# Two of eight pairs of the last batch's first product in seven block products, with changes at the start and the end

## The chip, the core and the metric

The kernel runs on one core of one Trainium2 chip. The core's engines each run their own instructions strictly in order and wait for each other by semaphores: TensorE (PE) multiplies matrices, VectorE (DVE) and ScalarE (ACT) do elementwise work, SyncE (SP) issues most of the transfers, and GpSimd (POOL) does next to nothing here. The metric is the device time of one execution in microseconds (us). The kernel before takes 2216.11 us, the median of three runs (2215.84 to 2216.43).

## The reference

Everything is float32; B is 4, N is 6080, C is 256, F is 2048.

```python
qn = q / (norm(q, axis=1) + 1e-6)          # q, k, v: (4, 6080, 256)
kn = k / (norm(k, axis=1) + 1e-6)
s  = kn.transpose(0, 2, 1) @ qn / tau      # (4, 256, 256): attention over channels
a  = softmax(s)                            # with 1e-9 added to the row sums
x  = (v @ a).reshape(24320, 256)
h  = maximum(x @ w_in, 0)                  # w_in: (256, 2048)
out = (h * h) @ w_out                      # w_out: (2048, 256)
```

## The kernel before

For each batch b the kernel first sums the 256 x 256 products of k and q over all rows (`Gram`), makes the softmax of it, and folds it into the input weights: W = a @ w_in (`softmax_and_W`). Then h = v @ W replaces two products. The weights of a batch are in four groups g of 512 columns; v comes in twelve blocks n of rows (ten of 512, two of 480).

Float32 operands are split into a high part that TensorE takes in one go and a low remainder (`_hi`, `_lo`), and each product is made of three: hi·hi, hi·lo, lo·hi. ACT makes the high part (a cast), DVE the low part (a subtraction).

The main loop (lines 798 to 849) runs over `steps` (b, n, f), with f one of 16 slices of 128 columns of h; two slices are a pair r (0 to 7). A step has `first_product` (lines 579 to 594): six matmuls of 512 columns into one of the three PSUM tiles of the pool `ps_h` (`bufs=3`, line 98), which ACT then empties by a relu into half of the tile `x` of the pair. Tiles of `x`, `g_hi` and `g_lo` have two buffers each. After the second step of a pair `squares_and_sums` (603) squares `x` on ACT, has DVE make four differences and sums of its quarters (slots 4 to 7), and splits slots 1 to 3 into `g_hi` and `g_lo`; one step later `parts_of_sums` (616) splits slots 4 to 7, ACT by a cast of 1024 columns and DVE by a subtraction of 1024.

The second product (h² @ w_out) is made two pairs later (`LAG = 2`): for blocks between the first two and the last (`by_seven`, 572) by seven products of 128 x 128 blocks instead of eight (`seven_products`, 651; sums of w_out are made once, in `sums_of_w_out`), nine matmuls of 256 columns in the pair's first step and twelve in its second. For the others it is `eight_products` (707). After a block's last pair ACT copies the two PSUM tiles `ps_o` (768 and 1024 columns) to SBUF, which frees them for the next block, DVE combines them over three later steps (`combine`), and SP stores them. Beside this, in each block, v of the next block is split (ACT at f = 6, DVE at f = 8) and v of the one after is loaded.

For the batches 1 to 3 the generator `attention_of_others` does the Gram products, softmax and W of the next batch piece by piece in between; during batch 3 nothing is left of that but the end of W. At the start `start_first` (310) loads nine chunks of q and k of batch 0 ahead on SP, TensorE sums their products, ACT squares them and DVE adds the squares up for the norms. The order that follows until the first W is written out by hand in `beside_first`, and `stages` times the decoding of the weights (they come as float64 and are decoded on ACT and DVE).

The lines on which the working turns are those that order a pair's work:

```python
if part == 0 and 0 <= i // 2 - 1 < len(pairs):
    parts_of_sums(*pairs[i // 2 - 1])
...
if part == 1 and i // 2 < len(pairs):
    squares_and_sums(*pairs[i // 2])
...
if i >= 2 * LAG:
    second_product(*pairs[i // 2 - LAG], part)
```

## Time and profile before

| | |
|---|---|
| median of three runs | 2216.11 us |
| the profiled execution | 2216.45 us |
| its span, first to last instruction | 2214.6 us |
| granted TensorE clock | 1.000 |
| ACT busy, share of the span | 83% |
| DVE busy, share of the span | 79% |
| transfers | 127 MB, 57 GB/s on average |

In the rows of the profile an engine's instructions are named by the tile written and the tiles read, with the shape as partitions x elements. All compute instructions carry line 27, that of a helper, so they are told apart by tile names. A timeline row begins with the start and the duration in us; in brackets stands the idle time ahead of it and what ended that. On ACT and DVE the recorded durations of independent neighbours overlap by some 0.1 us, so what an instruction takes of its engine is read from the distance of two starts.

### The profile page before, as it was taken

The numbers are of one execution on the slowest core, as the hardware profiler recorded it, in microseconds if no ns is written. First come the engines' busy times: TensorE is split into PE (matmuls) and PEld (weight loads), VectorE is DVE, ScalarE is ACT, GpSimd is POOL, SyncE is SP. The second block draws the span as 40 slices with busy tenths as digits, with TensorE's granted clock in tenths as the row PEclk, the third lists the DMA queues.
The fourth block names the chain that finished last, engine by engine and source line by source line (L and its number), as shares of the span: only waits on it lengthen the run. The fifth ranks groups of instructions, "written<-read, shape, count | busy, mean of one in ns | idle before, by whom it ended". The sixth has DMA issues, their size and how long they took to land.

```text
span 2214.6 us, 34388 instructions
## 1 busy us (share of the span) xinstructions
PE 2206.4 (100%) x13750; PEld 1982.2 (90%) x13750; DVE 1759.8 (79%) x2469; ACT 1842.3 (83%) x2294; POOL 0.7 (0%) x6
## 2 busy tenths in 40 slices
PE   9999999999999999999999999999999999999999
PEld 8788999989989999998998999998899888888898
DVE  6878888888778888878767888888877777777773
ACT  5788888888788888888878888888887888888885
POOL 0000000000000000000000000000000000000000
PEclk9999999999999999999999999999999999999999
DMA  9521122101111122110121222110102010010000
GB/s 342 179 77 38 60 75 67 46 19 38 57 67 58 61 70 70 55 41 22 36 76 48 69 64 69 58 53 23 37 20 76 21 37 20 22 36 20 22 26 18
DMA packets 76496, 127.01 MB, mean 57 GB/s; under 512 B 7728, under 2 KB 35120, under 8 KB 76336
## 3 DMA queue, kind: packets, MB, share of 16 engines
q1 hardware_dynamic: 76336, 124.81, 17.3%
q8 instruction: 108, 1.77, 0.3%
q14 instruction: 52, 0.43, 0.1%
HBM read 95.68 MB, written 29.10 MB: 56 GB/s over the span
## 4 chain that ended last, share of the span: by engine, by line
PE 98%; DVE 1%; DMA 0%; ACT 0%; issue 0%; SPq 0%; DVEq 0%
PE ps_h L27 47%; PE ps_o L27 43%; PE gram L27 6%; PE ps_w L27 2%; DVE dec_m L27 0%; DMA qk<-in_q 0%; DMA w_raw<-in_w_in 0%; PE ps_n L27 0%; DVE wi_lo L27 0%; ACT x L27 0%; ACT g_hi L27 0%; DVE w_lo L27 0%; PE ps_t L27 0%; PE ps_b L27 0%; DVE g_lo L27 0%
## 5 line engine op out<-in xcount | busy, mean ns | idle before, releaser
L27 DVE TENSOR_TENSOR g_lo<-x,g_hi 128x768 fp32r<-128x768 f32 (+2 forms) x744 | 804.2, 1081 | 97.2 <-ACT g_hi L27 96.5
L27 DVE TENSOR_TENSOR x<-x 128x256 f32<-128x256 f32 (+3 forms) x1080 | 550.8, 510 | 274.5 <-ACT x L27 249.1
L27 ACT CAST g_hi<-x 128x768 fp32r<-128x768 f32 (+2 forms) x744 | 697.8, 938 | 25.0 <-DVE x L27 12.2
L27 ACT ACTIVATE x<-ps_h 128x512 f32<-128x512 f32 (+1 forms) x768 | 455.7, 593 | 289.7 <-PE ps_h L27 266.0
L27 PE MATMUL ps_h<-v_hi,w_hi 128*128 128x512 f32 (+1 forms) x1536 | 478.5, 393 | 0.0
L27 PE MATMUL ps_h<-v_hi,w_lo 128*128 128x512 f32 (+1 forms) x1536 | 477.8, 392 | 0.0
L27 PE MATMUL ps_h<-v_lo,w_hi 128*128 128x512 f32 (+1 forms) x1536 | 475.0, 390 | 0.8 <-DVE v_lo L27 0.8
L27 ACT ACTIVATE x<-x 128x1024 f32<-128x1024 f32 (+1 forms) x384 | 404.4, 1053 | 11.9
L27 PE MATMUL ps_o<-g_lo,wS_hi 128*128 128x256 f32 (+1 forms) x1440 | 401.9, 279 | 0.0
L27 PE MATMUL ps_o<-g_hi,wS_lo 128*128 128x256 f32 (+1 forms) x1440 | 401.2, 279 | 0.0
L27 PE MATMUL ps_o<-g_hi,wS_hi 128*128 128x256 f32 (+1 forms) x1440 | 400.4, 278 | 0.0
L27 PEld LDWEIGHTS ps_h<-v_lo,w_hi 128*128 128x128 f32 x1536 | 287.8, 187 | 65.9 <-DVE v_lo L27 1.2
L27 PEld LDWEIGHTS ps_h<-v_hi,w_lo 128*128 128x128 f32 x1536 | 288.5, 188 | 62.4 <-DVE w_lo L27 0.3
L27 PE MATMUL ps_o<-g_hi,wo_hi 128*128 128x256 f32 (+3 forms) x1176 | 330.9, 288 | 0.0
L27 PE MATMUL ps_o<-g_hi,wo_lo 128*128 128x256 f32 (+3 forms) x1176 | 330.7, 288 | 0.0
L27 PE MATMUL ps_o<-g_lo,wo_hi 128*128 128x256 f32 (+3 forms) x1176 | 330.5, 288 | 0.0
L27 PEld LDWEIGHTS ps_o<-g_lo,wS_hi 128*128 128x128 f32 x1440 | 271.0, 188 | 15.9 <-DVE g_lo L27 0.2
L27 PEld LDWEIGHTS ps_o<-g_hi,wS_hi 128*128 128x128 f32 x1440 | 270.3, 188 | 15.5
L27 PEld LDWEIGHTS ps_o<-g_hi,wS_lo 128*128 128x128 f32 x1440 | 270.6, 188 | 0.0
L27 PEld LDWEIGHTS ps_h<-v_hi,w_hi 128*128 128x128 f32 x1536 | 238.9, 188 | 5.3
L27 PEld LDWEIGHTS ps_o<-g_hi,wo_hi 128*128 128x128 f32 x1176 | 221.5, 188 | 16.4
L27 PEld LDWEIGHTS ps_o<-g_lo,wo_hi 128*128 128x128 f32 x1176 | 220.8, 188 | 16.6 <-DVE g_lo L27 0.3
(90 smaller groups left out, 1668.1 us busy)
## 6 DMA issues: line engine op xcount, KB each, us to landing
qk<-in_k SPq DMA_DIRECT2D x87, 256.0 KB, 2.7
qk<-in_q SPq DMA_DIRECT2D x87, 256.0 KB, 3.0
v<-in_vT SPq DMA_DIRECT2D x40, 512.0 KB, 3.7
out_T<-o SPq DMA_DIRECT2D x152, 128.0 KB, 1.7
wi_hi<-wi_kept SPq DMA_DIRECT2D x12, 512.0 KB, 3.3
...
```

The lines of the kernel that those rows point to most:

```text
L27: return lambda *args, **kwargs: self.tc.keep_in_program_order(issue(*args, **kwargs))
```

## The change

In batch 3, for the blocks 2 to 10, the pairs r = 1 and r = 5 make their h by seven block products too. With v's block in quarters B and W's slice in quarters A, four sums S of the A and four sums T of the B are made, and the pair's two steps take 12 and 9 matmuls of 256 columns instead of 6 and 6 of 512. `sums_of_W` makes S once per pair (after W of batch 3 is done), `sums_of_v` and `parts_of_v_sums` make T for each block, a block ahead (at f = 8, 12, 14 and 15). The sums that such a product needs behind it are made in PSUM: ACT copies the first product out, and four DVE instructions add it and its followers up, before the second step's nine matmuls accumulate on top. For such a pair the order of the step changes: the pair before it has its differences made after this, and in the pair's second step the second product of an earlier pair comes first.

At the start, q's chunks 0 to 3 are issued by ACT instead of SP, tau is loaded after the chunks, and ACT's first activation (which loads its function table) comes behind its five transfers. In the first W the low part's products of both halves come last, with two pieces of the next batch's Gram ahead of them; in the later three W of batch 0 that second part comes behind the second product. v_lo of block 1 is made ahead of the weights' decoding. In the blocks 1 to 9 of batch 3, v_lo of the next block and the load behind it move from f = 8 to f = 13. At the end, the last block's sums lie in two PSUM tiles instead of one, the two copies go to separate SBUF tiles, and the second half is stored by ACT's queue.

```diff
@@ start @@
-    nc.sync.dma_start(tau_sb, tau.to_broadcast([P, 1]))
...
-    scalar.activation(const.tile([P, 1], F32, name="first"), exp_bias, AF.Square)
...
+            other = scalar if self.b == 0 and c < 4 else nc.sync
             for j0, j1 in pieces:
                 nc.sync.dma_start(raw[:p, 1, j0:j1, :], self.k[c][2][:, j0:j1, :])
-                nc.sync.dma_start(raw[:p, 0, j0:j1, :], self.q[c][2][:, j0:j1, :])
+                other.dma_start(raw[:p, 0, j0:j1, :], self.q[c][2][:, j0:j1, :])
...
         for c in range(AHEAD):
             load(c)
+        nc.sync.dma_start(tau_sb, tau.to_broadcast([P, 1]))
+        scalar.activation(const.tile([P, 1], F32, name="first"), exp_bias, AF.Square)
@@ softmax_and_W @@
-                for h, terms in ((0, (0, 1)), (1, (0,)), (0, (2,)), (1, (1, 2))):
+                for h, terms in ((0, (0, 1)), (1, (0, 1))):
                     products(h, terms)
                 yield
+                for h in range(NC):
+                    products(h, (2,))
                 for h in range(NC):
                     evict(h)
...
+        if b == B - 1:
+            for r in SEVEN_FIRST:
+                yield from sums_of_W(b, r)
+    SEVEN_FIRST, FIRST = (1, 5), 2
@@ the sums of v @@
+        if piece == 0:
+            vector.tensor_sub(S[:, 0:3:2, :], raw[:, :, half:tn], raw[:, 0, :tn].rearrange("p (k t) -> p k t", k=2))
+        else:
+            vector.tensor_sub(S[:, 1, :], raw[:, 1, half:tn], S[:, 0, :])
+            vector.tensor_sub(S[:, 3, :], raw[:, 1, 0:half], S[:, 1, :])
...
+        if part:
+            vector.tensor_sub(to, S, VS[b, n][1].bitcast(F32))
+        else:
+            scalar.copy(to, S)
@@ seven_first_products @@
+            for i, (wt, vt) in enumerate(((A[0], B_[0]), (A[0], B_[1]), (A[1], B_[0]))):
+                tensor.matmul(ps, wt, vt, start=start and i == 0, stop=stop and i == 2, skip_group_check=True)
...
+        if part == 0:
+            x = X[b, n, r] = pool.tile([P, 8, half], F32, tag="x", name=f"x{b}_{n}_{r}")
+            one, two = H[b, n, r] = [
+                ps_h.tile([P, 2, T // 2], F32, tag="h", name=f"ps_h{b}_{n}_{r}_{i}")[:, :, :half] for i in range(2)
+            ]
+            product(one[:, 0], "A11", "B11", start=True)
+            product(one[:, 1], "S2", "T2", stop=True)
+            product(two[:, 0], "S1", "T1", start=True)
+            product(two[:, 1], "S3", "T3")
+            P1, U4, U2 = (x[:, i, :] for i in (4, 5, 6))
+            scalar.copy(P1, one[:, 0])
+            vector.tensor_add(U2, one[:, 1], P1)
+            vector.tensor_add(U4, two[:, 0], U2)
+            vector.tensor_add(x[:, 3, :], two[:, 1], U4)
+            vector.tensor_add(two, two, x[:, 6:7, :].broadcast_to([P, 2, half]))
+        else:
+            product(one[:, 0], "A12", "B21", stop=True)
+            product(two[:, 0], "S4", "B22")
+            product(two[:, 1], "A22", "T4", stop=True)
+            scalar.activation(x[:, 3, :], x[:, 3, :], AF.Relu)
+            scalar.activation(x[:, 0, :], one[:, 0], AF.Relu)
+            scalar.activation(x[:, 1:3, :], two, AF.Relu)
@@ the end @@
+            tiles = [
+                ps_acc.tile([P, NC, T], F32, tag="o", name=f"ps_o{b}_{n}_{i}") for i in range(NC if final else 1)
+            ]
...
+            if last:
+                for tag, m, copy, queue in (("acc", 0, scalar.copy, nc.sync), ("dec", 1, vector.tensor_copy, scalar)):
+                    o = pool.tile([P, tn], F32, tag=tag, name=f"o{b}_{n}_{tag}", bufs=1)
+                    copy(o, psum[m])
+                    queue.dma_start(out[:, m, :], o)
+                return
@@ the main loop @@
+        chained, chain_next = (j < len(steps) and first_by_seven(*steps[j]) for j in (i, i + 1))
+        chain_next = chain_next and part == 1
+        if chained and part:
+            second_product(*pairs[i // 2 - LAG], part)
...
+            if i == 1:
+                split_v_lo(*order[1])
             for item in stages.get(i, ()):
                 weights.stage(item)
-            if i == 1:
-                split_v_lo(*order[1])
...
+        if chained and part == 0:
+            sums_and_parts(*pairs[i // 2 - 1])
         if part == 0 and 0 <= i // 2 - 1 < len(pairs):
             parts_of_sums(*pairs[i // 2 - 1])
-        if i in steps_of_W:
-            next(first)
         if part == 1 and i // 2 < len(pairs):
-            squares_and_sums(*pairs[i // 2])
+            squares(*pairs[i // 2])
+            if not chain_next:
+                sums_and_parts(*pairs[i // 2])
...
-        if i >= 2 * LAG:
+        if i >= 2 * LAG and not (chained and part):
             second_product(*pairs[i // 2 - LAG], part)
+        if i in steps_of_W:
+            next(first)
...
-            at_hi, at_lo = (None, None) if at == 0 else (12, 13) if at == 1 else (6, 8)
+            then = at + 1 < len(order) and has_sums(*order[at + 1])
+            at_hi, at_lo = (None, None) if at == 0 else (12, 13) if at == 1 else (6, 13) if then else (6, 8)
```

ACT's instructions of batch 3, block 5, from pair 0's second relu to pair 2's first, before. In the names 3_5_1 is batch 3, block 5, pair 1 (for `ps_h` the last number is the slice f, for `ps_o` and `o` there is only the block, and part 0 or 1); the number behind is that of the tile.

```order
L27 ACTIVATE x3_5_0_18843<-ps_h3_5_1_18856 128x512
L27 ACTIVATE x3_5_0_18843<-x3_5_0_18843 128x1024
L27 CAST g_hi3_5_0_18864<-x3_5_0_18843 128x768
L27 ACTIVATE x3_5_1_18891<-ps_h3_5_2_18884 128x512
L27 CAST g_hi3_5_0_18864<-x3_5_0_18843 128x1024
L27 COPY o3_4_18904<-ps_o3_4_0_18542 128x768
L27 ACTIVATE x3_5_1_18891<-ps_h3_5_3_18906 128x512
L27 ACTIVATE x3_5_1_18891<-x3_5_1_18891 128x1024
L27 CAST g_hi3_5_1_18914<-x3_5_1_18891 128x768
L27 COPY o3_4_18904<-ps_o3_4_1_18569 128x1024
L27 ACTIVATE x3_5_2_18942<-ps_h3_5_4_18935 128x512
```

The same stretch of ACT in the changed kernel; `ps_h3_5_1_0` and `ps_h3_5_1_1` are the two PSUM tiles of pair 1.

```order
L27 ACTIVATE x3_5_0_18983<-x3_5_0_18983 128x1024
L27 COPY x3_5_1_19017<-ps_h3_5_1_0_19018 128x256
L27 CAST g_hi3_5_0_19037<-x3_5_0_18983 128x768
L27 CAST g_hi3_5_0_19037<-x3_5_0_18983 128x1024
L27 COPY o3_4_19055<-ps_o3_4_0_18660 128x768
L27 COPY o3_4_19055<-ps_o3_4_1_18688 128x1024
L27 ACTIVATE x3_5_1_19017<-x3_5_1_19017 128x256
L27 ACTIVATE x3_5_1_19017<-ps_h3_5_1_0_19018 128x256
L27 ACTIVATE x3_5_1_19017<-ps_h3_5_1_1_19019 128x512
L27 ACTIVATE x3_5_1_19017<-x3_5_1_19017 128x1024
L27 CAST g_hi3_5_1_19083<-x3_5_1_19017 128x768
L27 ACTIVATE x3_5_2_19098<-ps_h3_5_4_19091 128x512
```

The two relus of 512 columns have become a copy ahead of pair 0's casts and three relus behind both copies of `ps_o`; between pair 0's two casts nothing else is left.

DVE at the same place, before: the last subtraction of block 4, then the sums and low parts of pair 0 and the sums of pair 1.

```order
L27 TENSOR_TENSOR g_lo3_4_7_18817<-x3_4_7_18795,g_hi3_4_7_18816 128x768
L27 TENSOR_TENSOR g_lo3_4_7_18817<-x3_4_7_18795,g_hi3_4_7_18816 128x1024
L27 TENSOR_TENSOR x3_5_0_18843<-x3_5_0_18843 128x512
L27 TENSOR_TENSOR x3_5_0_18843<-x3_5_0_18843 128x256 x2
L27 TENSOR_TENSOR g_lo3_5_0_18865<-x3_5_0_18843,g_hi3_5_0_18864 128x768
L27 TENSOR_TENSOR g_lo3_5_0_18865<-x3_5_0_18843,g_hi3_5_0_18864 128x1024
```

DVE there in the changed kernel; `vS1` is the low part of T, `vS0` its high part.

```order
L27 TENSOR_TENSOR g_lo3_4_7_18956<-x3_4_7_18931,g_hi3_4_7_18955 128x768
L27 TENSOR_TENSOR vS13_5_18974<-v_sums3_5_18777,vS03_5_18944 128x1024
L27 TENSOR_TENSOR g_lo3_4_7_18956<-x3_4_7_18931,g_hi3_4_7_18955 128x1024
L27 TENSOR_TENSOR x3_5_1_19017<-ps_h3_5_1_0_19018,x3_5_1_19017 128x256
L27 TENSOR_TENSOR x3_5_1_19017<-ps_h3_5_1_1_19019,x3_5_1_19017 128x256 x2
L27 TENSOR_TENSOR ps_h3_5_1_1_19019<-ps_h3_5_1_1_19019,x3_5_1_19017 128x512
L27 TENSOR_TENSOR x3_5_0_18983<-x3_5_0_18983 128x512
L27 TENSOR_TENSOR x3_5_0_18983<-x3_5_0_18983 128x256 x2
L27 TENSOR_TENSOR g_lo3_5_0_19038<-x3_5_0_18983,g_hi3_5_0_19037 128x768
L27 TENSOR_TENSOR g_lo3_5_0_19038<-x3_5_0_18983,g_hi3_5_0_19037 128x1024
```

Four instructions of pair 1 now stand ahead of the three sums of pair 0, on whose result ACT's cast of 1024 columns waits.

More of the change, by code (lines that the diff above doesn't have):

```diff
@@ L347, in rest @@
         def rest():
-            for c in range(g.n - LAST, g.n):
-                for _ in g.products(c, [(g.raws[c], g.raws[c])]):
-                    pass
+            for _ in first_products:
+                pass
             yield
@@ L544, in softmax_and_W, with blocks_of_W, sums_of_W @@
             yield
+        if b == B - 1:
+            for r in SEVEN_FIRST:
+                yield from sums_of_W(b, r)
+    SEVEN_FIRST, FIRST = (1, 5), 2
+    WS = {}
+    def blocks_of_W(b, r):
+        f0 = 2 * (r % PPG) * P
+        return [[[w[:, j, f0 + i * P : f0 + (i + 1) * P] for j in range(2)] for i in range(2)] for w in W[b, r // PPG]]
+    def sums_of_W(b, r):
+        f0 = 2 * (r % PPG) * P
+        hi, lo = (w[:, :, f0 : f0 + 2 * P].bitcast(F32) for w in W[b, r // PPG])
+        room = pool.tile([P, 2, NC, 2 * P], F32, tag="acc", name=f"w{b}_{r}", bufs=1)
+        w = room[:, 0]
+        S = room[:, 1].rearrange("p j (i m) -> p (j i) m", i=2)
+        vector.tensor_add(w, hi, lo)
+        yield
+        A11, A12, A21, A22 = (w[:, j, i * P : (i + 1) * P] for i in range(2) for j in range(2))
+        S1, S2, S3, S4 = (S[:, i] for i in range(4))
+        vector.tensor_add(S1, A21, A22)
+        vector.tensor_sub(S3, A11, A21)
+        yield
+        vector.tensor_sub(S2, S1, A11)
+        vector.tensor_sub(S4, A12, S2)
+        yield
+        both = pool.tile([P, 2, 4, P], F32R, tag="qk", name=f"WS{b}_{r}", bufs=QK_BUFS)
+        WS[b, r] = both[:, 0], both[:, 1]
+        scalar.copy(both[:, 0], S)
+        yield
+        vector.tensor_sub(both[:, 1], S, both[:, 0].bitcast(F32))
+        yield
     may_write_W = {(0, g) for g in range(NG)}
@@ L577, with has_sums, first_by_seven, seven_first_products @@
     G = {}
+    H = {}
+    def has_sums(b, n):
+        return b == B - 1 and FIRST <= n < NB - 1
+    def first_by_seven(b, n, f):
+        return has_sums(b, n) and f // 2 in SEVEN_FIRST
+    def seven_first_products(b, n, r, part):
+        half = blocks[n][1] // 2
+        _, v_hi, v_lo = V[b, n]
+        def product(ps, a, b_, start=False, stop=False):
+            A, B_ = W_of[a], v_of[b_]
+            for i, (wt, vt) in enumerate(((A[0], B_[0]), (A[0], B_[1]), (A[1], B_[0]))):
+                tensor.matmul(ps, wt, vt, start=start and i == 0, stop=stop and i == 2, skip_group_check=True)
+        A = blocks_of_W(b, r)
+        W_of = {f"A{i + 1}{j + 1}": [a[i][j] for a in A] for i in range(2) for j in range(2)}
+        W_of.update({f"S{i + 1}": [p[:, i, :] for p in WS[b, r]] for i in range(4)})
+        v_of = {
+            f"B{j + 1}{k + 1}": [v[:, j, k * half : (k + 1) * half] for v in (v_hi, v_lo)] for j in range(2) for k in range(2)
+        }
+        v_of.update({f"T{i + 1}": [p[:, i, :] for p in VS[b, n][1:3]] for i in range(4)})
+        if part == 0:
[14 more added lines that the diff above has]
+        else:
+            one, two = H.pop((b, n, r))
+            x = X[b, n, r]
+            product(one[:, 0], "A12", "B21", stop=True)
[4 more added lines that the diff above has]
+            scalar.activation(x[:, 1:3, :], two, AF.Relu)
@@ L709, in eight_products @@
         f = 2 * r + part
+        final = (b, n) == order[-1]
         if f == 0:
-            O[b, n] = ps_acc.tile([P, NC, T], F32, tag="o", name=f"ps_o{b}_{n}")
+            tiles = [
+                ps_acc.tile([P, NC, T], F32, tag="o", name=f"ps_o{b}_{n}_{i}") for i in range(NC if final else 1)
+            ]
+            O[b, n] = [tiles[m % len(tiles)][:, m, :tn] for m in range(NC)]
         hi, lo = (x.rearrange("p s t -> p (s t)")[:, part * tn : (part + 1) * tn] for x in G[b, n, r])
@@ L714, in eight_products @@
         order_of = [(i, m) for i in range(3) for m in range(NC)]
-        last = (b, n, f) == steps[-1]
+        last = final and f == NF - 1
         if last:
@@ L729, in eight_products @@
         if f == NF - 1:
-            o = pool.tile([P, NC, tn], F32, tag="o_sb", name=f"o{b}_{n}", bufs=1)
             at = b * N + t0
@@ L846 @@
                     load_v(*order[at + 2])
+            if then and f in (14, 15):
+                parts_of_v_sums(*order[at + 1], f - 14)
         if i >= PAIR and part:
```

50 lines of the change are left out of this document (34 added, 16 removed).

## The prediction

> **What bounds the kernel now.** I read the page first: its span, its busy times and its chain of waits.
>
> ```profile
> span 2214.6 us, 34388 instructions
> PE 2206.4 (100%) x13750; PEld 1982.2 (90%) x13750; DVE 1759.8 (79%) x2469; ACT 1842.3 (83%) x2294; POOL 0.7 (0%) x6
> PE 98%; DVE 1%; DMA 0%; ACT 0%; issue 0%; SPq 0%; DVEq 0%
> ```
>
> TensorE is busy all the time and is 98% of the chain: each matmul less is a gain, so long as the others keep up. They have to be asked in the stage that is changed, batch 3 from about 1750 us on. TensorE's timeline there gives the pace; below are the first rows of four stretches that follow each other.
>
> ```profile
> 1800.71 0.28 PE L27 MATMUL ps_o<-g_hi,wo_hi 128*128 128x256 f32 x1
> ...
> 1801.77 0.62 PE L27 MATMUL ps_h<-v_hi,w_hi 128*128 128x512 f32 x2
> ...
> 1803.15 0.28 PE L27 MATMUL ps_o<-g_hi,wS_hi 128*128 128x256 f32 x1
> ...
> 1804.55 0.40 PE L27 MATMUL ps_h<-v_hi,w_hi 128*128 128x512 f32 x1
> ```
>
> The distance of starts tells the cost, as durations overlap: nine matmuls of 256 columns take 1.06 us, six of 512 take 1.38, twelve of 256 take 1.40, so 0.117 for 256 columns and 0.231 for 512. A pair is 2 x 1.38 + 1.06 + 1.40, about 5.24 us with rounding, a block of eight 41.9.
>
> Then ACT's and DVE's timelines over some pairs of the same stage.
>
> ```profile
> 1787.65 0.60 ACT L27 ACTIVATE x<-ps_h 128x512 f32<-128x512 f32 x1 [0.81 <-PE ps_h L27]
> 1788.29 1.06 ACT L27 ACTIVATE x<-x 128x1024 f32<-128x1024 f32 x1
> 1789.38 0.83 ACT L27 CAST g_hi<-x 128x768 fp32r<-128x768 f32 x1
> 1790.45 0.60 ACT L27 ACTIVATE x<-ps_h 128x512 f32<-128x512 f32 x1 [0.23 <-PE ps_h L27]
> 1791.03 1.05 ACT L27 CAST g_hi<-x 128x1024 fp32r<-128x1024 f32 x1
> 1792.89 0.60 ACT L27 ACTIVATE x<-ps_h 128x512 f32<-128x512 f32 x1 [0.81 <-PE ps_h L27]
> ...
> 1797.21 0.79 ACT L27 COPY o<-ps_o 128x768 f32<-128x768 f32 x1
> ...
> 1800.58 1.01 ACT L27 COPY o<-ps_o 128x1024 f32<-128x1024 f32 x1
> 1801.49 0.60 ACT L27 ACTIVATE x<-ps_h 128x512 f32<-128x512 f32 x1
> ...
> 1807.68 1.04 ACT L27 CAST v_hi<-v 128x1024 fp32r<-128x1024 f32 x1
> 1808.63 0.59 ACT L27 ACTIVATE x<-ps_h 128x512 f32<-128x512 f32 x1
> ```
>
> ```profile
> 1789.38 1.61 DVE L27 TENSOR_TENSOR x<-x 128x512 f32<-128x512 f32 x3 [1.28 <-ACT x L27]
> 1790.91 0.95 DVE L27 TENSOR_TENSOR g_lo<-x,g_hi 128x768 fp32r<-128x768 f32 x1
> 1792.11 1.23 DVE L27 TENSOR_TENSOR g_lo<-x,g_hi 128x1024 fp32r<-128x1024 f32 x1 [0.25 <-ACT g_hi L27]
> ...
> 1813.53 1.22 DVE L27 TENSOR_TENSOR g_lo<-x,g_hi 128x1024 fp32r<-128x1024 f32 x1
> 1814.66 1.22 DVE L27 TENSOR_TENSOR v_lo<-v,v_hi 128x1024 fp32r<-128x1024 f32 x1
> ```
>
> ACT waits for TensorE twice in a pair, 0.81 and 0.23. Without these waits a pair has a shortest round, which hangs on both engines: relu to square 0.64, square to DVE's three sums 1.09, sums 1.61, and only then ACT's cast of 1024, which holds ACT 0.95 (from the v_hi row to the next). That is **4.3 us against TensorE's 5.24**: behind by some delay, ACT makes up 0.9 in each pair. The block's extras are two copies of ps_o (0.7 and 0.91) and v_hi (0.95). So before, ACT's round of a block is 8 x 4.3 + 2.6 = 37.0 of 41.9: room of 4.9 us.
>
> **The seven products, on TensorE.** For a pair r = 1 or 5, twelve matmuls of 512 columns (2.77 us) give way to 21 of 256 (2.45): 0.32 us. Nine blocks with two pairs each: 18 x 0.32 = **-5.8 us**. A block is then 41.3.
>
> **The seven products, on ACT and DVE.** Not in the trace are ACT's copies and relus of 256 columns out of PSUM and DVE's adds that read and write PSUM. The nearest rows are these.
>
> ```profile
> L27 ACT COPY o<-ps_o 128x512 f32<-128x512 f32 x4 | 2.1, 586 | 0.0
> L27 ACT ACTIVATE s<-s,negmax 128x256 f32<-128x256 f32 x8 | 4.0, 500 | 0.9 <-DVE negmax L27 0.9
> L27 DVE TENSOR_TENSOR eT_lo<-ps_t,eT_hi 128x512 fp32r<-128x512 f32 x4 | 2.8, 691 | 0.1
> L27 DVE TENSOR_TENSOR x<-x 128x256 f32<-128x256 f32 x608 | 258.4, 425 | 20.8
> ```
>
> From 512 to 1024 columns ACT's copy grows by 0.42, so 256 take about 0.37 (at most the 0.50 of the second row). A DVE subtraction from PSUM takes 0.69, which is also what the first of the three sums leaves of 1.61 after two of 0.425, so I take 0.42 for 256 columns and 0.69 for the 512 written back to PSUM.
>
> What counts is not these durations but where they stand. In ACT's new order the copy of 256 follows pair 0's square, and pair 0's cast of 1024 waits for three sums that DVE now makes behind four instructions of pair 1. These four depend on each other and on the copy: 3 x 0.42 + 0.69 + 3 x 0.04 = 2.1 us. I count from pair 0's second relu (0): square 0.64 to 1.7, copy to 2.0, the four to 4.1, the three sums to 5.6, the cast to 6.65. From the cast of 768 (done by 2.7) to 5.6 ACT has nothing it may do: behind the waiting cast stand both copies of ps_o and pair 1's relus, and TensorE waits for the PSUM tiles that these set free. Then three relus (0.27 + 0.27 + 0.64), square at 7.7, sums to 10.4, cast, and the next relu at 11.4. **Two pairs take 11.4 instead of 8.6.**
>
> A block of ACT is then 4 ordinary pairs (17.2), 2 x 11.4 = 22.8, the old extras 2.6 and the high part of v's sums 0.95: 43.5 us. DVE's additions come in its way at three places: the low part of v's sums (1.13) delays the subtraction that frees pair 1's tile x (0.55), v's first sum of the next block and the combining stand ahead of the four in pair 5 (0.6), and v's later sums ahead of pair 6's (0.4). That makes **45.1 us against TensorE's 41.3**, so ACT and DVE bound these blocks, and the saving on TensorE is lost.
>
> How it reaches TensorE: in block 2 ACT is still on time. In pair 1 TensorE, counted from its first product, needs the emptied ps_o at 6.3 and the emptied first tile at 7.4, and ACT gives them at 6.35 and 7.8: 0.5 us. ACT is then 2.6 us late, makes up 3 x 0.9 less v_hi's 0.95 until pair 5, where the four adds end about 1.1 us after TensorE wants to add to their tile, and 0.1 us more is lost at a low part: 1.2. So block 2 costs 1.7 - 0.64 = +1.1. From block 3 on ACT never catches up: 45.1 - 41.9 = +3.2 each for seven blocks, 22.4, and about +2.8 for block 10 with 480 columns. **Sum: +26.** Without the three collisions (1.55 a block) it would be 14, with 0.3 more for each pair's new instructions 31.
>
> Making S once per pair of weights (two adds, a copy and a subtraction of 512 columns, four adds of 256) costs DVE some 3 us each, spread over steps ahead of block 2. The later row is from there:
>
> ```profile
> 1800.00:1840.00 40.00, 40.00 (x252) 35.85 (x251) 31.66 (x46) 33.48 (x42) 0.00 (x0) 1.00 0.09 27
> ...
> 1740.00:1760.00 20.00, 20.00 (x130) 18.04 (x129) 13.86 (x20) 16.75 (x21) 0.00 (x0) 1.00 0.00 1
> ```
>
> (columns: stretch, length, busy PE, its weight loads, DVE, ACT, POOL, then clock, DMA share, GB/s). DVE has 6 of 20 us free there, so I take nothing; at worst a late tile costs 1 us once. The later load of v lands within a few us and has nine steps of 2.6 before it is read: nothing.
>
> **The start.** The issues on SP and TensorE's Gram in the timeline, then two stretches of 1 us with what the transfers moved:
>
> ```profile
> 0.74 0.38 SPq L106 DMA_DIRECT2D tau_sb<-in_tau  x1
> 1.18 0.42 SPq L267 DMA_DIRECT2D qk<-in_k  x1
> ...
> 3.54 0.44 SPq L268 DMA_DIRECT2D qk<-in_q  x1
> ...
> 8.73 39.09 PE L27 MATMUL gram<-qk 128*128 128x256 f32 x180 [1.48 <-DMA qk<-in_q]
> ```
>
> ```profile
> 4.00:5.00 1.00, 1.00 (x4) 0.69 (x4) 0.00 (x0) 0.00 (x0) 0.00 (x0) 1.00 0.67 150
> ...
> 9.00:10.00 1.00, 1.00 (x6) 0.88 (x5) 0.24 (x1) 0.76 (x2) 0.00 (x0) 1.00 1.03 391
> ```
>
> From 8.73 TensorE runs 39 us without a stop, and what it waits for is q's chunk 1, the sixth of SP's issues (3.54). The issues are 0.47 apart; with tau behind and q's on ACT, chunk 1's q is the third of ACT's queue, issued some 1.8 us earlier. But between 4 and 9 us the engines move less than the 391 GB/s later, and not each dip need be want of issues. Tau's place alone (0.44) is the least, the full 1.8 of earlier issue the most; I take **-1.3**, in the upper half because two thirds of that bandwidth lie idle in the worst dip. The earlier Gram also needs the squares' additions to come earlier, which follow the same transfers. ACT's table load moves behind five issues; its first square waits for chunk 0 anyhow.
>
> The Trainium skill's page "DMA: Bandwidth & Descriptors", section "Issuing engines are not separate DMA queues", says that a second issuing engine saves only the time of issuing, since all transfers share the same 16 engines. By that, up to 1.8 us of issue are to be had and none of the bandwidth; the trace agrees in so far as the engines are not full until 9 us, and a term of -1.8 would move the sum by half a us.
>
> **The first W and the end.** TensorE's waits, and ACT's and DVE's last copies:
>
> ```profile
> PE ps_h L27 <- DVE v_lo L27: 0.8, 1, 0.8
> PE ps_w L27 <- DVE wi_lo L27: 0.5, 1, 0.5
> ```
>
> ```profile
> 2210.33 0.56 ACT L27 COPY o<-ps_o 128x480 f32<-128x480 f32 x1 [3.94 <-PE ps_o L27]
> ...
> 2210.93 0.66 DVE L27 COPY o<-ps_o 128x480 f32<-128x480 f32 x1 [3.34 <-ACT o L27]
> ```
>
> v_lo ahead of the decoding and W's last part behind the second product take away 1.3 at best. Against it, a piece of Gram that stood between the first W and h stands ahead now, so TensorE waits there for ACT's w_hi, up to 1 us. I take **-0.5**, between -1.3 and +1. At the end DVE need not wait for ACT's copy: **-0.6**, the transfer behind it unchanged. In return block 11 needs both tiles of ps_o at once instead of one: 0 to 1 us, **+0.2**, as ACT has the sums of only one kind of pair less there and catches up.
>
> **The sum**, from the profiled execution's own 2216.45 us (0.3 over the median shown): 2216.45 + 26 - 1.3 - 0.5 - 0.6 + 0.2 = about **2240 us**.
>
> **Rivals.** *The waits stay hidden* (faster): ACT's added work is 0.6 us a seven pair and 0.95 a block, so its busy time rises from 35.1 a block (33.48 of 40) to some 37 of 41.3, DVE's from 33.2 to about 39.8. If three PSUM tiles and two of each SBUF tile carry ACT over its empty 2.9 us, only the saving is left: 2216.45 - 5.8 - 1.3 - 0.5 - 0.6 + 0.1 = 2208.4. It decides where ACT's round falls below 41.3, that is with 1.9 us less per seven pair. For it speaks that neither engine is full; against it that each row of the walk is a wait in program order, which a spare buffer doesn't shorten.
>
> The Trainium skill's page "Perfetto Trace Analysis", section "Identifying the Most-Contended Engine", calls occupancy a fair measure for ACT and DVE of how near they are to their limit. By that rule this rival holds, since both stay under 97%; but in this case's rows DVE stands idle 1.28 and 0.25 in each pair, both times for ACT, and such waits in a round of two engines are in no occupancy.
>
> *ACT catches up in each block* (same): the stall is that of pair 1 alone, 9 x 0.5 = 4.5: 2208.4 + 4.5 = 2212.9. It needs the adds in PSUM to be done 1 us sooner than I count. *The 21 matmuls are no faster*, if 256 columns took 0.132 there: 5.8 more on TensorE, but then ACT's bound hides it; no time of its own.
>
> **How the numbers follow.** My forecast has 0.66, with a range of its own from 2227 (no collisions) to 2247 (dearer new instructions). The hidden waits have 0.22, ACT catching up 0.12. A measurement of this kernel can tell about 0.2% (4.4 us) from no change: faster below 2211.7, slower over 2220.5. So faster 0.22, same 0.12, slower 0.66. To leave out no more than 2 in 10 the range must reach into the faster case: 2208 to 2247.
>
> **What would show it.** In the blocks 3 to 9 the distance of equal rows of TensorE should be about 45 us; in pair 0 of each, ACT should sit idle some 2.9 us ahead of its cast of 1024 for DVE, and TensorE's waits name ACT's x and DVE's ps_h. If TensorE has no waits after 1800 us and the blocks are 41.3 apart, the walk is wrong. Chunk 1's Gram should start near 7.4 and not 8.73, DVE's last copy near the last matmul.

## The result, and the profile after

| | before | after |
|---|---|---|
| median of the runs | 2215.98 us (2215.45 to 2216.43, 4 runs) | 2249.23 us (2248.14 to 2249.49, 4 runs) |
| profiled run, its span | 2216.45, 2214.6 us | 2249.34, 2247.5 us |
| ratio after to before | | 1.0148, 95% interval 1.0136 to 1.0160 |

The change makes the kernel 1.5% slower, 33 us; the forecast was 24 (2240 us, range 2208 to 2247). The direction and the mechanism were right; the size lies outside the range, because block 2, the round of a block and the changes ahead of the blocks were each priced too low.

The page of the kernel after: span, busy times and the shares of the chain of waits.

```profile
span 2247.5 us, 34867 instructions
PE 2214.8 (99%) x13912; PEld 1987.1 (88%) x13912; DVE 1818.0 (81%) x2589; ACT 1846.4 (82%) x2341; POOL 0.7 (0%) x6
PE 85%; DVE 8%; ACT 6%; DMA 1%; issue 0%; ACTq 0%; DVEq 0%; SPq 0%
```

TensorE's share of the chain falls from 98% to 85%, though "busy" still says 99%: its busy time is 8.4 us longer than before, with less to multiply, so the profile records part of its waiting as busy. What it waits for is in the list of TensorE's waits of the kernel after (total us, times, longest):

```profile
PE ps_h L27 <- DVE v_lo L27: 7.8, 8, 1.0
PE ps_o L27 <- ACT o L27: 7.6, 9, 0.9
PE ps_h L27 <- DVE ps_h L27: 6.8, 9, 1.1
...
PE ps_h L27 <- ACT x L27: 1.8, 9, 0.2
PE ps_o L27 <- ACT g_hi L27: 1.4, 1, 1.4
```

The four that come 8 or 9 times stand once in each block with seven products (a "seven block" from here on); before, these blocks had none of them. Together they are 24.0 us, less than is lost: at the pace read below, eight blocks lose 4 us each against TensorE's own 41.3. Where they come from is seen in ACT's timeline around pairs 0 and 1 of block 4:

```profile
1888.44 0.37 ACT L27 COPY x<-ps_h 128x256 f32<-128x256 f32 x1 [0.56 <-DVE g_lo L27]
1888.71 0.84 ACT L27 CAST g_hi<-x 128x768 fp32r<-128x768 f32 x1
1892.53 1.05 ACT L27 CAST g_hi<-x 128x1024 fp32r<-128x1024 f32 x1 [2.99 <-DVE x L27]
1893.49 1.70 ACT L27 COPY o<-ps_o 128x768 f32<-128x768 f32 x2
1895.09 0.42 ACT L27 ACTIVATE x<-x 128x256 f32<-128x256 f32 x1
1895.40 0.87 ACT L27 ACTIVATE x<-ps_h 128x256 f32<-128x256 f32 x2
```

and in DVE's for the same time:

```profile
1888.84 1.41 DVE L27 TENSOR_TENSOR x<-ps_h,x 128x256 f32<-128x256 f32 x3 [0.49 <-ACT x L27]
1890.29 0.70 DVE L27 TENSOR_TENSOR ps_h<-ps_h,x 128x512 f32<-128x512 f32 x1
1890.90 1.60 DVE L27 TENSOR_TENSOR x<-x 128x512 f32<-128x512 f32 x3
```

ACT stands still for 2.99 us ahead of pair 0's cast of 1024; meanwhile DVE does pair 1's four adds (2.06 from 1888.84) and only then pair 0's three sums. The copies of ps_o and pair 1's relus stand behind the waiting cast, and TensorE needs the tiles that they empty. ACT's pace is read from ACT's copies of 256 columns, of pair 1 in blocks 2, 3 and 10:

```profile
1797.57 0.37 ACT L27 COPY x<-ps_h 128x256 f32<-128x256 f32 x1 [0.42 <-PE ps_h L27]
...
1843.00 0.37 ACT L27 COPY x<-ps_h 128x256 f32<-128x256 f32 x1 [0.56 <-DVE g_lo L27]
...
2160.80 0.36 ACT L27 COPY x<-ps_h 128x240 f32<-128x240 f32 x1 [0.57 <-PE ps_h L27]
```

Eight blocks in 363.2 us are 45.40 us each, and the very first takes 45.43.

In the lead-in, TensorE's timeline of the kernel after shows the first W and the first product with w_out, which waits for ACT where before it did not:

```profile
62.56 1.27 PE L27 MATMUL ps_w<-wi_lo,eT_hi 128*128 128x512 f32 x4
64.14 1.08 PE L27 MATMUL ps_h<-v_hi,w_hi 128*128 128x512 f32 x2 [0.32 <-ACT w_hi L27]
...
73.91 0.73 PE L27 MATMUL ps_o<-g_hi,wo_hi 128*128 128x512 f32 x2 [1.38 <-ACT g_hi L27]
```

### The profile page after: what moved, and what is told of

The parts are those of the page before. It is cut to its first block, busy times and chain, and to the rows that moved or that the text cites. A ratio compares the mean times of both kernels' runs of the same rounds, so it can differ in the third digit from the quotient of the medians.

```text
span 2247.5 us, 34867 instructions
## 1 busy us (share of the span) xinstructions
PE 2214.8 (99%) x13912; PEld 1987.1 (88%) x13912; DVE 1818.0 (81%) x2589; ACT 1846.4 (82%) x2341; POOL 0.7 (0%) x6
## 4 chain that ended last, share of the span: by engine, by line
PE 85%; DVE 8%; ACT 6%; DMA 1%; issue 0%; ACTq 0%; DVEq 0%; SPq 0%
PE ps_h L27 41%; PE ps_o L27 37%; PE gram L27 5%; DVE x L27 4%; ACT x L27 3%; PE ps_w L27 2%; ACT g_hi L27 2%; DVE g_lo L27 2%; DMA qk<-in_q 1%; ACT o L27 1%; DVE acc L27 1%; DVE v_sums L27 0%; DVE v_lo L27 0%; DVE o L27 0%; ACT v_hi L27 0%
## 5 line engine op out<-in xcount | busy, mean ns | idle before, releaser
L27 ACT ACTIVATE x<-ps_h 128x512 f32<-128x512 f32 (+2 forms) x768 | 449.1, 587 | 234.1 <-PE ps_h L27 212.4
L27 PE MATMUL ps_h<-v_lo,w_hi 128*128 128x512 f32 (+2 forms) x1500 | 463.5, 388 | 7.8 <-DVE v_lo L27 7.8
L27 PE MATMUL ps_h<-v_hi,w_hi 128*128 128x512 f32 (+2 forms) x1500 | 468.8, 391 | 2.2 <-ACT x L27 1.8
L27 PE MATMUL ps_h<-v_hi,w_lo 128*128 128x512 f32 (+2 forms) x1500 | 466.1, 389 | 0.0
L27 ACT ACTIVATE x<-x 128x1024 f32<-128x1024 f32 (+3 forms) x402 | 411.6, 1024 | 11.9
L27 PEld LDWEIGHTS ps_h<-v_lo,w_hi 128*128 128x128 f32 x1500 | 280.3, 187 | 73.5 <-DVE v_lo L27 11.2
L27 PEld LDWEIGHTS ps_h<-v_hi,w_lo 128*128 128x128 f32 x1500 | 281.8, 188 | 59.2
L27 PEld LDWEIGHTS ps_h<-v_hi,w_hi 128*128 128x128 f32 x1500 | 233.9, 188 | 9.8 <-ACT x L27 3.6
```

Source lines behind the costliest of these rows:

```text
L27: return lambda *args, **kwargs: self.tc.keep_in_program_order(issue(*args, **kwargs))
```

## The experiments

Theory A: the order on ACT and DVE in pairs 0/1 and 4/5 makes their round of a block longer than TensorE's, and the loss is there. Rivals: the amount of work, the matmuls of 256 columns, v_lo's move, or the start. Behind each run's edit stands what was expected of it; the cuts of code show the lines that matter.

### The two halves apart: no_seven and only_seven

no_seven takes the pairs out of the changed kernel:

```
-    SEVEN_FIRST, FIRST = (1, 5), 2
+    SEVEN_FIRST, FIRST = (), 2
     def has_sums(b, n):
-        return b == B - 1 and FIRST <= n < NB - 1
+        return False
```

only_seven puts the changed start, W order and end back to those of before and keeps the pairs.

> The changed kernel with no pair of seven products and none of the sums made for them; its start, its first W and its end stay as changed. Theory A (the round of ACT and DVE in the seven pairs, 45.4 us a block against the 41.9 before, costs some 31 us): what is left is the lead-in, 2.9 us later in the trace of the changed kernel, less 0.5 at the end, so about 2218.4 us. Rival (the loss comes from the start or is a general slowing): well over 2225 us.

> The kernel before with the two pairs of seven products alone; start, first W and end as before. Theory A: the two parts of the change add up, so 2216.0 + 31 = about 2247 us, blocks 3 to 9 at 45.4 us each. Rival (the seven pairs suffer from what the start or the W order does to them): clearly under 2245 us.

no_seven: 2218.83 us (10 runs, 1.0013 of before, 1.0004 to 1.0022). only_seven: 2247.12 us (1.0141, 1.0124 to 1.0158). The seven products cost 31.2 us (2247.12 - 2215.88, the median of before beside it); the rest of the change costs 3.0.

### Order or work: no_adds and sums_first

no_adds leaves out ACT's copy of the first product and the four adds; one DVE copy of 256 columns stands in their place:

```
-            scalar.copy(P1, one[:, 0])
-            vector.tensor_add(U2, one[:, 1], P1)
-            vector.tensor_add(U4, two[:, 0], U2)
-            vector.tensor_add(x[:, 3, :], two[:, 1], U4)
-            vector.tensor_add(two, two, x[:, 6:7, :].broadcast_to([P, 2, half]))
+            vector.tensor_copy(x[:, 3, :], two[:, 1])
```

sums_first issues the three sums of the pair ahead at another place and nothing else:

```
             scalar.copy(P1, one[:, 0])
+            sums_of_h(*pairs[pairs.index((b, n, r)) - 1])
             vector.tensor_add(U2, one[:, 1], P1)
...
-            sums_and_parts(*pairs[i // 2 - 1])
+            sums_and_parts(*pairs[i // 2 - 1], summed=True)
```

> The changed kernel without ACT's copy of the first product and with one DVE copy of 256 columns (some 0.42 us) in the place of the four adds that follow each other (2.1 us): the sums of the products of h are left out, everything else is issued as before. Theory A (DVE's chain stands ahead of pair 0's sums): two pairs of a block fall by 2 x 1.7 us at least, the block from 45.4 to 42.1 or to TensorE's own 41.3, so 2212 to 2220 us. Rival (the 21 products of 256 columns or v_lo's later place cost the time): 2245 us or more, the block still over 45 us.

> The changed kernel with the same instructions in another order: DVE makes pair 0's three sums ahead of the four adds of the seven pair, and ACT's copy of the first product stays ahead of the cast of 768. Theory A (order, not work): the adds end 1.3 us later but the cast of 1024 no longer waits for them; two pairs take some 10.6 us rather than 11.4, a block 1.6 less than 45.4, so about 2235 us (2230 to 2241). Rival (the sum of the work on ACT and DVE sets the pace): no change, 2249 us.

no_adds: 2215.94 us. ACT's copies of ps_o (its timeline) stand 41.69 us apart:

```profile
1801.11 1.71 ACT L27 COPY o<-ps_o 128x768 f32<-128x768 f32 x2
...
1842.80 1.71 ACT L27 COPY o<-ps_o 128x768 f32<-128x768 f32 x2
```

This is 2.9 us under no_seven: without the adds the loss is gone. In TensorE's timeline of no_adds, the starts of pair 5's matmuls and of what follows them are

```profile
1858.90 0.28 PE L27 MATMUL ps_h<-v_hi,w_hi 128*128 128x256 f32 x1
...
1860.32 0.28 PE L27 MATMUL ps_o<-g_hi,wo_hi 128*128 128x256 f32 x1
...
1862.80 0.28 PE L27 MATMUL ps_h<-v_hi,w_hi 128*128 128x256 f32 x1
...
1863.86 0.63 PE L27 MATMUL ps_h<-v_hi,w_hi 128*128 128x512 f32 x2
...
1865.26 0.28 PE L27 MATMUL ps_o<-g_hi,wo_hi 128*128 128x256 f32 x1
```

So 21 matmuls of 256 columns take 1.42 + 1.06 = 2.48 us, and twelve of 512 take 2 x 1.40: 0.32 us less a pair. TensorE is nearly the bound again. It still loses 0.3 us a block ahead of the next block's first matmul that reads v_lo, which DVE ends only then.

sums_first: 2222.95 us (1.0032, 1.0020 to 1.0044), 26.3 us less than the change with the same instructions. Its ACT timeline at pair 1, and TensorE's wait that is left in the seven blocks:

```profile
1839.85 1.05 ACT L27 CAST g_hi<-x 128x1024 fp32r<-128x1024 f32 x1 [0.36 <-DVE x L27]
1840.80 1.75 ACT L27 COPY o<-ps_o 128x768 f32<-128x768 f32 x2
...
1883.18 1.75 ACT L27 COPY o<-ps_o 128x768 f32<-128x768 f32 x2
```

```profile
PE ps_h L27 <- DVE ps_h L27: 4.0, 9, 1.1
```

The cast waits 0.36 and not 2.99; a block takes 42.38. I had expected 1.6 us a block and got 3.05: I let the adds' later end lengthen the round one for one, while the round came down to about 1 us over TensorE's own 41.3, in which TensorE still waits for the adds. So most of the loss is the order and not the sum of the work.

### What a wait doesn't tell, and a point of turning: v_lo_early and one_pair

```
v_lo_early:
-            ... else (12, 13) if at == 1 else (6, 13) if then else (6, 8)
+            ... else (12, 13) if at == 1 else (6, 8)
one_pair (seven products in pair 5 alone):
-    SEVEN_FIRST, FIRST = (1, 5), 2
+    SEVEN_FIRST, FIRST = (5,), 2
```

> The changed kernel with v_lo of the next block made in step 8 again, not 13. TensorE's waits name v_lo with 7.8 us in all, the dearest line. Theory A (the round of ACT and DVE sets the block's 45.4 us, and the wait for v_lo is only where one eighth of it shows): another wait takes its place, 2247 to 2251 us. Rival (v_lo's move costs what its wait shows): 7.8 us less, 2241.5 us.

> The changed kernel with seven products in pair 5 alone. Theory A (a round of ACT and DVE against TensorE's): six ordinary pairs of 4.3, 11.4 for pairs 4 and 5, 2.6 and 0.95 for the extras and about 1.2 of collisions make 41.9 us a block against TensorE's 41.65: nearly all of the 31 us goes, 2218 to 2224 us. Rival (each seven pair costs its own 1.7 us): half the loss, about 2234 us.

v_lo_early: 2257.46 us (1.0189, 1.0172 to 1.0206): 8.2 slower, where one theory had no change and the other a gain. The waits for v_lo are gone, but in ACT's timeline at pair 5

```profile
1918.26 1.05 ACT L27 CAST g_hi<-x 128x1024 fp32r<-128x1024 f32 x1 [4.14 <-DVE x L27]
```

the cast waits 4.14 us, 1.1 longer than in the changed kernel (3.01 there): v_lo's 1.13 now stand ahead of the four adds, and a block takes 46.56 us. That is the round again, which my expectation had forgotten to walk for the new place. In this execution the granted clock is down at 0.66 on the mean of 5 us in two of the blocks, but those blocks are no longer than the others.

one_pair: 2224.26 us (1.0038, 1.0023 to 1.0053), 5.4 over no_seven. One pair of two costs a sixth of the loss and not half: with one, a block is 1 us over TensorE's own 41.65; with two, 4 us over its 41.3. My 41.9 us a block is 42.6 from the third block on; v_lo, left out of that walk too, keeps TensorE waiting for 5.1 us in all.

### The 3 us ahead of the seven blocks: w_back, q_back, tau_back, end_alone

All but end_alone start from no_seven, and each puts one part back to the code of before: W's order (with v_lo and the later pieces), q's loads on SP, tau's load and the first activation ahead of the loads. end_alone is the kernel before with the changed end.

```
w_back:
-                for h, terms in ((0, (0, 1)), (1, (0, 1))):
+                for h, terms in ((0, (0, 1)), (1, (0,)), (0, (2,)), (1, (1, 2))):
q_back:
-            other = scalar if self.b == 0 and c < 4 else nc.sync
+            other = nc.sync
tau_back, behind the loop over load(c):
-        nc.sync.dma_start(tau_sb, tau.to_broadcast([P, 1]))
-        scalar.activation(const.tile([P, 1], F32, name="first"), exp_bias, AF.Square)
```

> The kernel without the seven products (no_seven, 2218.8 us), and the first W's order, v_lo's place and W's later pieces put back to those of before; start and end stay as changed. Theory B (the new W order costs the 1.5 us by which the first relu stands later behind the norms' matmuls, 18.2 against 16.7): first relu 16.7 to 16.8 us behind ps_n again, 2217.3 us or, if the later drift of the blocks belongs to it too, 2216. Rival (the start costs it): unchanged within 0.4 us.

> no_seven with all loads of q on SP again (tau still behind the loads, W order and end as changed). Theory B (ACT's queue brings the Gram forward by some 0.8 us on the mean of the four traces with it, 46.4 to 48.0 against 47.6): 0 to 1 us slower than no_seven's 2218.8 us. Rival (sharing the transfers between two queues costs time): 0.5 us or more faster. The slow drift of the blocks (they grow 0.1 us each in the last stage) goes if ACT's queue causes it.

> The kernel before with the changed end alone (two PSUM tiles in the final block, the copies side by side, the last transfer on ACT's queue). If the end is worth what the trace shows, 0.5 us under before: 2215.4 us, and blocks of 41.86 us as before. If the slow drift (41.97 a block in no_seven) belongs to the end, some 1 to 2 us over that.

> no_seven (2218.83 us) with tau's load and ACT's first activation back ahead of the loads; q's first chunks stay on ACT, W order and end as changed. Neither the W order put back (w_back 2218.18) nor q put back (q_back 2218.14) took the lead-in's 2.9 us away, and the slow growth of the blocks is in both and not in end_alone (2215.41). Theory C (tau and the first activation behind the loads carry the growth of some 2 us): blocks of the last stage as before, 2216.5 to 2217.3 us. Rival (the growth belongs to any two of the three, or to none): unchanged within 0.5 us.

| kernel | median us | range, 10 runs |
|---|---|---|
| no_seven | 2218.83 | 2217.93 to 2219.21 |
| w_back | 2218.18 | 2217.32 to 2218.88 |
| q_back | 2218.14 | 2217.89 to 2218.65 |
| tau_back | 2216.49 | 2216.23 to 2217.08 |
| end_alone | 2215.41 | 2214.92 to 2215.97 |

The end gives its 0.6 us (2216.04 is the median of before beside it). The runs alone can't tell this step from nothing (ratio 0.9988 to 1.0006), but the traces show it: DVE's last copy starts 3.90 us behind the start of the last g_lo in end_alone, and 4.50 before. W's new order costs: the first relu comes 18.24 us behind ps_n (the matmuls of the norms, which follow the first Gram) in no_seven and 16.82 in w_back, of which 0.65 is left at the end, with ranges that overlap. The rows are from TensorE's and then ACT's timeline of no_seven,

```profile
46.83 0.35 PE L27 MATMUL ps_n<-ones,acc 128*128 128x1 f32 x2
```

```profile
65.07 0.60 ACT L27 ACTIVATE x<-ps_h 128x512 f32<-128x512 f32 x1 [1.52 <-PE ps_h L27]
```

and from TensorE's and then ACT's of w_back:

```profile
48.14 0.35 PE L27 MATMUL ps_n<-ones,acc 128*128 128x1 f32 x2 [0.15 <-DVE acc L27]
```

```profile
64.96 0.60 ACT L27 ACTIVATE x<-ps_h 128x512 f32<-128x512 f32 x1 [1.75 <-PE ps_h L27]
```

The ps_n rows show too why one execution says little about the start: it begins between 46.43 and 48.14 us in the ten profiles with q on ACT, mean 47.30, and between 46.58 and 47.79 in the ten with q on SP, mean 47.27. ACT's queue gives nothing; q_back is 0.7 us faster, with ranges that overlap. What tau_back takes away is the greatest part, 2.3 us, and there no wait of that size goes: the blocks of the last batch are 41.87 us again and not 41.97, and many of those ahead of them are shorter by less (46.33 for 46.36).

### Where a tile lies: shift_alone and first_placed

The change gives out the tile "first" behind wo_hi and wo_lo, so in the built program these begin at byte 17,600 of each partition and not at 17,632. shift_alone is end_alone with this alone, no instruction moved; first_placed is no_seven with the tile in its old place, tau and activation still late.

```
shift_alone:
-    scalar.activation(const.tile([P, 1], F32, name="first"), exp_bias, AF.Square)
     wo_hi = const.tile([P, NF, C], F32R, name="wo_hi")
     wo_lo = const.tile([P, NF, C], F32R, name="wo_lo")
+    scalar.activation(const.tile([P, 1], F32, name="first"), exp_bias, AF.Square)
first_placed:
+    first_room = const.tile([P, 1], F32, name="first")
     wo_hi = ...
...
-        scalar.activation(const.tile([P, 1], F32, name="first"), exp_bias, AF.Square)
+        scalar.activation(first_room, exp_bias, AF.Square)
```

> end_alone (2215.41 us) with the tile first given out behind wo_hi and wo_lo, so that both begin 32 bytes earlier (17600 instead of 17632 in each partition); every instruction of every engine stands where it stood. Theory D (wo's place makes the second product's matmuls slower): blocks of the last stage 41.97 us instead of 41.87, 2217.3 us. Rival (the moved instructions do it): 2215.4 us.

> no_seven (2218.83 us) with tau's load and the first activation behind the loads as changed, but the tile first given out ahead of wo_hi, which then begins at 17632 as before. Theory D: 2216.5 us, blocks of 41.87. Rival (the moved instructions do it): 2218.8 us, 41.97.

shift_alone: 2217.90 us, 2.5 over end_alone. first_placed: 2216.36, 2.5 under no_seven. ACT's copies of ps_o, four blocks apart, of shift_alone

```profile
1797.71 0.79 ACT L27 COPY o<-ps_o 128x768 f32<-128x768 f32 x1
...
1965.60 0.79 ACT L27 COPY o<-ps_o 128x768 f32<-128x768 f32 x1
```

and of first_placed

```profile
1796.86 0.79 ACT L27 COPY o<-ps_o 128x768 f32<-128x768 f32 x1
...
1964.33 0.79 ACT L27 COPY o<-ps_o 128x768 f32<-128x768 f32 x1
```

give 41.97 and 41.87 us a block. So the place is the cause, both ways. Which matmuls become slower by it, and why 32 bytes count, was not tried.

### Could it pay: spread, pool_sums, best_a, best_b, late_one, late_two

```
spread (on sums_first, W order of before):
-            if then and f in (8, 12):        sums_of_v(..., f // 12)
+            if then and f in (5, 7):         sums_of_v(..., f // 7)
-            ... (6, 13) if then ...          parts in steps 14, 15
+            ... (6, 12) if then ...          parts in steps 13, 14
pool_sums (sums_first, start and W of before): combine and sums_of_v
-        vector.tensor_add(...) / vector.tensor_sub(...)
+        pool_engine.tensor_add(...) / pool_engine.tensor_sub(...)
best_a / best_b (as pool_sums, all sums on DVE): SEVEN_FIRST = (5,), sums_of_v in steps 10, 12 / 12, 13
late_one / late_two (best_a, SEVEN_FIRST = (5,) / (1, 5)):
-            vector.tensor_add(two, two, x[:, 6:7, :].broadcast_to([P, 2, half]))
...
+            vector.tensor_add(x[:, 1:3, :], two, x[:, 6:7, :].broadcast_to([P, 2, half]))
+            scalar.activation(x[:, 1:4, :], x[:, 1:4, :], AF.Relu)
```

> sums_first (2222.95 us) with the W order of before and the sums of v moved out of pairs 4 to 6: its differences in pairs 2 and 3, v_lo in pair 6, the parts of the sums in pairs 6 and 7. Theory A: the two stalls left in a block (TensorE's second product of part 1 waits for the adds in PSUM, 0.34 in pair 1 and 0.63 in pair 5) shrink below 0.2 together, a block takes 41.4 to 41.6 rather than 42.38, and W gives 1.5: 2213 to 2216 us. Rival (DVE's work of 38.2 us a block is the bound whatever its order): 2220 us or more.

> Start and W order of before, the changed end, seven products in the order of sums_first, and both the differences of v and the combining of the output's sums (some 4 us a block) on POOL instead of DVE. Theory A: what is left in sums_first is DVE's want of time around pairs 1 and 5 (0.97 us a block of TensorE's waits); with 4 us less of it the waits go, a block takes 41.4 us, and the time is 2215.4 - 9 x 0.6 = 2210 us. Rival (POOL's work slows DVE's or arrives late): blocks over 42 us, 2216 us or more.

> Start and W order of before, the changed end, seven products in pair 5 alone with pair 0's kind of sums first (the three sums of pair 4 ahead of the four adds), the differences of v in steps 10 and 12. Theory A: DVE has some 36 us of work in a block of 41.55 and no pair ahead of pair 5 with extras, so TensorE's wait for the adds stays under 0.1 us and its saving of 0.32 a block shows: 2215.4 - 9 x 0.3 = 2212.7 us. Rival (the adds come 0.6 us late in pair 5 even so, as in sums_first): 2215.5 to 2218.5 us.

> best_a with v's differences in steps 12 and 13, so that nothing but pair 5's own work stands behind its adds. Theory A: as best_a or 0.5 us better, 2212 to 2213 us; if the parts of the sums come late for pair 0's v_lo, TensorE waits there up to 1 us a block, 2215 to 2220 us.

> best_a (2216.68 us, blocks of 41.88) with the sum U2 no longer added in PSUM ahead of TensorE's last two products but behind them, on the way from PSUM to x, in front of one relu of 768 columns; the low part of pair 4's sums goes behind it. TensorE then waits for three adds (1.3 us) and not for four (2.0). Theory A (the wait is the loss): it goes, a block takes 41.87 - 0.32 = 41.55, and with nine blocks 2216.7 - 9 x 0.28 = 2214.2 us, 0.08% under the kernel before, hardly more than can be told. Rival (the later relu makes ACT and DVE late elsewhere): 2216.5 us or more.

> late_one with both pairs, 1 and 5. Theory A with room (the waits of 0.34 and 0.63 of sums_first go): blocks of 41.3 us, 2211 us. Theory A without room (DVE's 38.2 us of work and two lengthened rounds leave waits of 0.3 to 0.7 a block): 41.6 to 42.0 us, 2213 to 2217 us. Rival (the total of the work bounds): 2220 us or more.

| kernel | median us | ratio to before, 95% |
|---|---|---|
| spread | 2223.74 | 1.0034, 1.0021 to 1.0047 |
| pool_sums | 2250.01 | 1.0153, 1.0138 to 1.0168 |
| best_a | 2216.68 | 1.0004, 0.9995 to 1.0012 |
| best_b | 2217.94 | 1.0009, 1.0000 to 1.0018 |
| late_one | 2217.49 | 1.0007, 0.9998 to 1.0016 |
| late_two | 2221.36 | 1.0024, 1.0015 to 1.0033 |

spread: pair 1's stall went, but that of pair 5 grew; a block takes 42.56 us. TensorE's timeline at pair 5 now shows

```profile
1863.61 0.38 PE L27 MATMUL ps_h<-v_hi,WS 128*128 128x256 f32 x1 [0.79 <-DVE ps_h L27]
```

against 0.37 in sums_first. That the work put into pair 3 did it is likely and not shown. pool_sums: the groups of POOL (whole execution) and of DVE's sums (1780 to 2200 us) in it,

```profile
L27 POOL TENSOR_TENSOR o<-o 128x256 f32<-128x256 f32 (+3 forms) x225 | 310.5, 1380 | 1865.6 <-ACT o L27 1851.5
```

```profile
L27 DVE TENSOR_TENSOR x<-x 128x256 f32<-128x256 f32 (+3 forms) x224 | 137.7, 615 | 52.7 <-ACT x L27 47.6
```

and DVE's sums in sums_first in the same stage

```profile
L27 DVE TENSOR_TENSOR x<-x 128x256 f32<-128x256 f32 (+3 forms) x225 | 114.9, 511 | 36.3 <-ACT x L27 30.2
```

POOL takes 1.38 us on the mean for adds that DVE does in about half a us: 1.24 for 0.42 at 256 columns, 1.66 for 0.69 at 512. DVE's own sums grow from 511 to 615 ns beside it. The growth falls just where POOL is at work. In block 3, POOL's timeline and then DVE's rows of a pair's three sums are

```profile
1845.02 7.16 POOL L27 TENSOR_TENSOR o<-o 128x512 f32<-128x512 f32 x5 [33.68 <-ACT o L27]
1852.14 2.28 POOL L27 TENSOR_TENSOR v_sums<-v 128x512 f32<-128x512 f32 x1
1854.50 1.95 POOL L27 TENSOR_TENSOR v_sums<-v,v_sums 128x256 f32<-128x256 f32 x2
```

```profile
1847.15 2.46 DVE L27 TENSOR_TENSOR x<-x 128x512 f32<-128x512 f32 x3 [1.13 <-ACT x L27]
1853.19 3.54 DVE L27 TENSOR_TENSOR x<-x 128x512 f32<-128x512 f32 x3
1860.38 1.61 DVE L27 TENSOR_TENSOR x<-x 128x512 f32<-128x512 f32 x3 [1.31 <-ACT x L27]
```

The three sums take 2.46 and 3.54 us beside POOL, and 1.61 once it has ended.

best_a: TensorE's matmuls of one pair now start

```profile
1861.08 0.28 PE L27 MATMUL ps_h<-v_hi,w_lo 128*128 128x256 f32 x1
1861.37 0.39 PE L27 MATMUL ps_h<-v_hi,WS 128*128 128x256 f32 x1
```

0.29 apart in place of 0.12, and the next start is 0.1 late too: 0.28 lost of 0.32 saved, a block of 41.88. best_b, with v's differences two steps and one later, has 42.04. late_one removes that wait, and 0.42 us appear ahead of the next block's first matmul that reads v_lo, as in no_adds; a block takes 42.08. In late_two the wait is v_lo's, some 0.4 a block (TensorE's timeline):

```profile
1873.49 0.73 PE L27 MATMUL ps_h<-v_lo,w_hi 128*128 128x512 f32 x2 [0.43 <-DVE v_lo L27]
```

In none of these six kernels, nor in sums_first, do the pairs gain. No run gives the orders of late_one and late_two an earlier v_lo, so whether that would pay is open. Not one kernel here is faster than before by more than can be told; end_alone is nearest, at 0.9997 (0.9988 to 1.0006).

## Why the prediction was right and where it was wrong

The time lies outside the range although the mechanism was right. The terms that failed are block 2 (+1.1), the round of a block (45.1), the start (-1.3), the first W (-0.5), and the moved load of tau with the first activation, which was counted at nothing.

**The seven products on TensorE (-0.32 a pair): right.** no_adds' rows give it, and best_a's loss of 0.28 nearly eats it.

**The order as the cause, and its signs: right.** ACT's empty 2.9 us is 2.99; the four adds' 2.1 us is 2.06; 0.37, 0.42 and 0.69 us for the unseen operations came as 0.37, 0.42 and 0.70. The distance of blocks is 45.40 to 45.43 for 45.1. DVE's busy time is 38.2 of 45.4 us in the changed kernel and 38.0 of 42.4 in sums_first: the same work at two paces. The Trainium skill's page "Perfetto Trace Analysis", section "Identifying the Most-Contended Engine", calls occupancy a fair measure of how near ACT and DVE are to their limit. Read as the first rival reads it, that did not hold here: DVE was busy 84% of a block and ACT 79%, and yet their round set the pace. So the first rival fell, and ACT catching up in each block fell with it.

**"Block 2 costs +1.1": wrong, about 2 us too little.** I walked block 2 from an ACT that is still on time and counted TensorE's stalls inside it as 1.7. On ACT the period from its pair 1 to block 3's is 45.43 already. On TensorE it is 44.77, from the first matmul of pair 1 to that of the next block:

```profile
1796.67 0.28 PE L27 MATMUL ps_h<-v_hi,w_hi 128*128 128x256 f32 x1
...
1841.44 0.28 PE L27 MATMUL ps_h<-v_hi,w_hi 128*128 128x256 f32 x1
```

That is 2.9 over 41.87. By the distances of starts TensorE loses 1.0 us in pair 1, where I had 0.5, some 1.1 in pair 5 as forecast, and 1.2 ahead of block 3's pair 1, where I had 0.1. There it waits for v_lo (TensorE's timeline of the kernel after),

```profile
1836.57 0.72 PE L27 MATMUL ps_h<-v_lo,w_hi 128*128 128x512 f32 x2 [0.98 <-DVE v_lo L27]
```

whose move from step 8 to step 13 the sum left out. The wait is where the lateness comes out, not the price of the move: with v_lo back in step 8, v_lo_early's blocks are longer still. Counted by ACT's round, 45.40 - 41.87 for all eight blocks is 28.3 us, where 1.1 + 22.4 stood: 2.1 from block 2 counted like the others, 2.7 from the round being 0.3 longer than 45.1.

**The start (-1.3): wrong, nothing.** The bandwidth in the dip did lie idle, but ten profiles against ten show ps_n no earlier. Chunk 1's Gram starts at 8.05 here and at 7.48 in sums_first, which has the same start, but at 7.33 in late_one, which has the old one; and the Gram's end doesn't follow it. By the Trainium skill's page "DMA: Bandwidth & Descriptors", section "Issuing engines are not separate DMA queues", a second issuing engine saves only the time of issuing, here 1.8 us at most by the prediction's estimate; no run here shows any of it.

**Tau and the first activation behind the loads (counted at nothing): wrong, 2.5 us.** Not by their time but by their tile's place. In the seven blocks, where TensorE waits anyhow, some 0.8 of it (8 x 0.1) should be hidden in the change: only_seven, with the old place, has blocks of 45.43 us too.

**The first W (-0.5, up to +1): wrong in sign.** The first relu comes 1.4 later; W's last products stand together behind Gram, and ACT's w_hi waits for them. In TensorE's list of waits those for v_lo (0.8) and wi_lo (0.5) went, as forecast. In their place came 0.3 for w_hi, which I had allowed for, and 1.4 for g_hi at the first product with w_out, which I had not. In w_back the two old waits are there again and the two new ones are not. By the medians 0.65 of the delay lasts, with ranges that overlap.

**The end (-0.6): right** by the traces (3.90 for 4.50). Block 11's +0.2 has no run of its own.

Together: the profiled times differ by 2249.34 - 2216.45 = 32.9 us, forecast 23.8. only_seven's profiled run, at 2247.14, parts the missing 9.1 in two: the seven products took 30.7 for 26.2, and the rest of the change 2.2 for -2.4, nearly all of it in the lead-in (ACT's copy in pair 1 of block 2 starts at 1797.57, in only_seven at 1794.94). The range failed since its upper end was put down to the seven products alone. Their dear case of 31 covers the 30.7, but gives a sum of about 2245 us; up to 2247 that left less than 2 us for a lead-in that came 4.6 dearer than forecast.
